# Attention, two expert layers: the query tiles of the second batch loaded as 32 by 32 squares and transposed on VectorE

## The chip, the core and the metric

The kernel runs on one core of a Trainium2 chip. The metric is the device time of one execution in microseconds (us). Below, PE is TensorE (matmuls and transposes through the identity matrix), PEld its weight loads, DVE is VectorE, ACT is ScalarE, POOL is GpSimd, and SP is SyncE, the engine from whose queue all loads and stores are issued.

## What is computed

A block-sparse attention over q, k, v of shape (2, 8, 768, 64) is followed by a mixture of eight experts with Sinkhorn-normalised gates and by a second layer with a rational activation. The change lies in the attention alone:

```python
k_sum = k.reshape(B, H, nb, block, D).max(axis=3)          # block = 32
v_sum = v.reshape(B, H, nb, block, D).mean(axis=3)
scores_l = scale * np.matmul(q, k.transpose(0, 1, 3, 2))   # kept where |i - j| < 16
scores_s = scale * np.einsum('bhsd,bhnd->bhsn', q, k_sum) + np.log(block)
a = softmax(np.concatenate([scores_l_masked, scores_s], axis=-1))
attn = np.matmul(a, np.concatenate([v, v_sum], axis=2))
x = attn.transpose(0, 2, 1, 3).reshape(B * S, H * D)
x = _moe_ref(x, w_gate, w1, w2)
return _moe2_ref(x, w_in, w_out, a, b)
```

All is float32, and `scale` is 1/8.

## The kernel before

**Steps.** The attention goes through 24 steps `t` (`NQ`), each 64 queries of all 8 heads; steps 0 to 11 are the first batch, 12 to 23 the second. A step has five pieces, issued at different times: `scores(t)` (q times k on PE, lines 626 and 637), `exps(t)` (ACT), `norm(t)` (DVE), `trans(t)` (PE transposes the weights, line 668; ACT copies them, line 670) and `values(t)` (weights times v, line 687). Up to step 11 the loop takes one step at a time and ends it with `values(t - 3)`; from step 12 on `pair(s)` takes two, with `values(s - 4)` and `values(s - 3)` directly behind the scores of `s` and `s + 1`. So `values(14)` and `values(15)` stand in pair 18.

**Between the pieces** stand pieces of the first expert unit's matmuls (`main`, lines 184 to 186) and whatever the table `todo` lists for the step: `at(s, f, ...)` puts `f` into step `s`. Every engine, SP too, takes its instructions in the order in which this code issues them; nothing is reordered.

**The v rows of a step** come through `load_vx(t)` into one of three buffers `vx[t % 3]`. It is issued when `values(t - 3)` has read that buffer. In pair 16, after `values(12)` and `values(13)`, this loads the rows of steps 15 and 16.

**A query tile** is 256 tokens of one batch, four steps' worth: (b, i) with i from 0 to 2. PE wants it with the 64 head dimensions on the partitions, two heads to a 128-row slab, four slabs: `qs`, 128 by 4 by 256. Before, a tile of the second batch is loaded by `load_tok` in two DMAs (even and odd tokens, rows of 64 floats), and `prep_q` makes eight PE transposes into two PSUM buffers of tag "tr" (`transpose8`, line 427) and copies both out with the scale 1/8 (`place`, lines 438 and 440: one on ACT, one on DVE). Tile (1, 0) is loaded with step 7 into `accs` and prepared with step 10, (1, 1) with steps 11 and 14, (1, 2) with steps 15 and 18:

```python
at(11, load_tok, q, "q", 1, 1)
at(15, load_tok, q, "q", 1, 2)
at(7, load_tok, q, "q", 1, 0, 0)
order += [(j * TPL - 2, "q", j // NL, j % NL) for j in range(2, NQ // TPL)]
```

The keys are prepared in the same way by `prep_k`, from tiles that POOL has first rewritten by token (`by_token`, line 388).

Of the kernel before, what the change touches and what calls it, by code (L numbers as in the profile page):

```python
# [10 lines left out]
F32 = mybir.dt.float32  # L11
# [11 lines left out]
def kernel(  # L23
# [14 lines left out]
    nc = tc.nc  # L38
    B, H, S, D = q.shape
    NT, DM = out.shape  # L40
    NE, _, FE = w1.shape
    F2 = w_out.shape[0]
    P = 128
# [18 lines left out]
    NP = H // 2  # L62
    LT = 2 * P
    NL = S // LT
# [30 lines left out]
    accs = xpool.tile([P, NTT, DM], F32, name="accs")  # L95
# [270 lines left out]
    with ExitStack() as actx:  # L366
        apool = actx.enter_context(tc.tile_pool(name="att", bufs=2, side="right"))
# [11 lines left out]
        nat = {}  # L379
        kT = {}  # L380
        ks = {}
        vs = {}
        qT = {}
# [34 lines left out]
        def transpose8(nm, b, i, par, early=False):  # L418

            t = nat[nm, b, i]  # L420
            name = f"{nm}ps_{b}_{i}_{par}"
            if early or par:
                ps = psm.tile([P, NP * P], F32, tag="mm", name=name).rearrange("p (c n) -> p c n", c=NP)
            else:
                ps = psa.tile([P, NP, P], F32, tag="tr", name=name, bufs=2)
            for p in range(NP):
                nc.tensor.transpose(ps[:, p, :], t[par][:, p * P:(p + 1) * P], ident)
            return ps

        def place(dst, par, ps, mul, early=False):  # L430

            if len(dst.shape) == 4:
                o = dst.rearrange("p s c (n t) -> p s c n t", t=2)[:, :, :, :, par]
                ps = ps.rearrange("p c (s n) -> p s c n", s=TPL)
            else:
                o = dst.rearrange("p c (n t) -> p c n t", t=2)[:, :, :, par]
            if par and not early:
                nc.vector.tensor_scalar_mul(o, ps, mul)
            else:
                nc.scalar.mul(o, ps, mul)  # L440
# [28 lines left out]
        def new_k(b, i):  # L469
            a = slot(b * QB + i * TPL)  # L470
            kT[b, i] = kw[:, a:a + TPL, :, WIN:WIN + QT]
            if i == 0:
                ks[b] = apool.tile([P, NP, NB], F32, tag="ks", name=f"ks_{b}")

        def new_q(b, i):
            qT[b, i] = qs[(b * NL + i) % 2]
# [19 lines left out]
            nc.vector.tensor_max(o, o, m)  # L496

        qscale = 1.0 / math.sqrt(D)

        ordered = []  # L500

# [23 lines left out]
        def prep_k(b, i):  # L525
            new_k(b, i)
            for par in range(2):
                place(kT[b, i], par, transpose8("k", b, i, par), 1.0, i == 0)

        def prep_q(b, i):  # L530
            new_q(b, i)
            for par in range(2):
                place(qT[b, i], par, transpose8("q", b, i, par), qscale, (b, i) == (0, 2))

# [264 lines left out]
        def at(s, f, *args):  # L799
            todo.setdefault(s, []).append(lambda: f(*args))  # L800
# [19 lines left out]
        at(5, by_token, "q", 0, 2)  # L820
        for i in range(NL):
            at(6 + i, by_token, "k", 1, i)
        at(11, load_tok, q, "q", 1, 1)
        at(15, load_tok, q, "q", 1, 2)
        at(7, load_nat, v, "v", 1, 0)
        at(8, load_nat, v, "v", 1, 1)
        at(9, load_nat, v, "v", 1, 2, 8)
        at(5, dma_w, 0, 2, 0, 6)
        at(7, dma_w, 0, 2, 1)
        at(7, load_tok, q, "q", 1, 0, 0)  # L830
        for t in range(1, 3):
            at(3, block_values, t)
        order = [(7 + i, "k", 1, i) for i in range(NL)]
# [2 lines left out]
        for t, nm, b_, i_ in order:  # L836
            at(t, prep_q if nm == "q" else prep_k, b_, i_)
# [72 lines left out]
        for s in range(PAIR):  # L910
# [11 lines left out]
            if s == AV:  # L922
                trans(1)
                exps(3)
                norm(2)
                prep_v(0, 2)
                prep_q(0, 1)
# [111 lines left out]
    for src, dst in ((w_in, f_in), (w_out, f_out)):  # L1039
        rows, cols = dst[0].shape[0] // P, dst[0].shape[1]  # L1040
        flat, o = rows * cols, 0
        while o < flat:
            e = min(o + CW, flat)
            parts = []
            while o < e:
                r, c = divmod(o, cols)
# [458 lines left out]
```

## Time and profile before

| what | before |
|---|---|
| median of 3 runs (lowest to highest) | 1350.45 us (1350.25 to 1350.63) |
| the profiled execution, its time | 1350.37 us |
| its span, first to last instruction | 1348.7 us |
| PE busy | 1340.8 us, 99% of the span |
| DVE, ACT, POOL busy | 1050.1, 510.6, 803.1 us |
| granted TensorE clock | 1.00 |
| chain that ended last | PE 97%, DVE 1%, ACT 1%, DMA 1% |

Busy time is the time in which an engine had an instruction under way, from first to last of them merged. The chain is followed back from the last instruction, at each step to what released it. The profiled execution lasted 1.67 us longer than its span (what lies before the first and behind the last instruction), and its time is 0.08 us under the median.

### The profile page before, as it was taken

The numbers are of one execution on the slowest core, as the hardware profiler recorded it, in microseconds if no ns is written. First come the engines' busy times: TensorE is split into PE (matmuls) and PEld (weight loads), VectorE is DVE, ScalarE is ACT, GpSimd is POOL, SyncE is SP. The second block draws the span as 40 slices with busy tenths as digits, with TensorE's granted clock in tenths as the row PEclk, the third lists the DMA queues.
The fourth block names the chain that finished last, engine by engine and source line by source line (L and its number), as shares of the span: only waits on it lengthen the run. The fifth ranks groups of instructions, "written<-read, shape, count | busy, mean of one in ns | idle before, by whom it ended". The sixth has DMA issues, their size and how long they took to land.

```text
span 1348.7 us, 20280 instructions
## 1 busy us (share of the span) xinstructions
PE 1340.8 (99%) x7343; PEld 1186.2 (88%) x7343; DVE 1050.1 (78%) x1956; ACT 510.6 (38%) x1136; POOL 803.1 (60%) x983
## 2 busy tenths in 40 slices
PE   8999999999999999999999999999999999999999
PEld 6888898999899999899999999999999888888887
DVE  7766588777777777777787777777777689988885
ACT  7875213222222222222222222222222379866662
POOL 7625747777767777777777767777777012222221
PEclk9999999999999999999999999999999999999999
DMA  9730112222222222222222222222221411312102
GB/s 263 169 85 1 63 35 73 78 77 73 68 73 68 69 76 69 83 70 85 69 81 67 71 70 68 77 68 83 68 86 56 146 60 45 94 33 94 32 16 78
DMA packets 122004, 102.40 MB, mean 76 GB/s; under 512 B 36272, under 2 KB 102960, under 8 KB 121904
## 3 DMA queue, kind: packets, MB, share of 16 engines
q1 hardware_dynamic: 121904, 101.10, 25.4%
q8 instruction: 58, 0.95, 0.3%
q14 instruction: 42, 0.34, 0.1%
HBM read 81.15 MB, written 19.92 MB: 75 GB/s over the span
## 4 chain that ended last, share of the span: by engine, by line
PE 97%; DVE 1%; ACT 1%; DMA 1%; SPq 0%; issue 0%; POOL 0%; DVEq 0%
PE p_v L185 12%; PE p_v L184 12%; PE p_v L186 12%; PE p L184 8%; PE p L186 8%; PE p L185 8%; PE X L1280 6%; PE X L1278 6%; PE X L1279 6%; PE Z L1280 3%; PE Z L1279 3%; PE Z L1278 3%; PE Y L1280 2%; PE Y L1279 2%; PE Y L1278 2%; PE xo L687 1%
## 5 line engine op out<-in xcount | busy, mean ns | idle before, releaser
L1393 DVE SCALAR_TENSOR_TENSOR accs<-p_v,Pt,accs 128x512 f32<-128x512 f32 x336 | 244.2, 745 | 86.8 <-PE p_v L186 86.0
L184 PE MATMUL p_v<-w2h_v,hh_v 128*128 128x512 f32 x720 | 282.0, 392 | 0.1
L186 PE MATMUL p_v<-w2h_v,hl_v 128*128 128x512 f32 x720 | 281.7, 391 | 0.0
L185 PE MATMUL p_v<-w2l_v,hh_v 128*128 128x512 f32 x720 | 281.6, 391 | 0.0
L1287 DVE SCALAR_TENSOR_TENSOR hl_v<-s,hh_v 128x384 fp32r<-128x384 f32 x180 | 135.9, 755 | 76.1 <-ACT hh_v L1286 74.6
L234 POOL TENSOR_TENSOR hl<-ta,hh 128x512 fp32r<-128x512 f32 x48 | 62.4, 1300 | 204.5 <-ACT hh L233 153.1
L1298 ACT COPY s<-X 128x384 f32<-128x384 f32 x56 | 27.0, 483 | 407.5 <-PE X L1280 407.5
L1087 POOL TENSOR_SCALAR ce<-ce 128x296 uint32<-128x296 uint32 (+1 forms) x56 | 67.1, 1199 | 177.5 <-DVE ce L1078 177.5
L186 PEld LDWEIGHTS p_v<-w2h_v,hl_v 128*128 128x128 f32 x720 | 135.1, 188 | 28.4
L184 PEld LDWEIGHTS p_v<-w2h_v,hh_v 128*128 128x128 f32 x720 | 135.4, 188 | 26.4 <-DVE accs L1388 0.5
L185 PEld LDWEIGHTS p_v<-w2l_v,hh_v 128*128 128x128 f32 x720 | 135.2, 188 | 26.1
L1286 ACT ACTIVATE hh_v<-s 128x384 fp32r<-128x384 f32 x180 | 94.9, 527 | 125.9 <-DVE s L1321 67.8
L110 POOL TENSOR_TENSOR wS<-S,wS 128x256 fp32r<-128x256 f32 x120 | 100.2, 835 | 14.4 <-ACT wS L107 4.7
L184 PE MATMUL p<-xh,w1h 128*128 128x512 f32 (+2 forms) x272 | 101.2, 372 | 0.0
L186 PE MATMUL p<-xh,w1l 128*128 128x512 f32 (+2 forms) x272 | 99.1, 364 | 0.0
L185 PE MATMUL p<-xl,w1h 128*128 128x512 f32 (+2 forms) x272 | 99.0, 364 | 0.0
L184 PE MATMUL p<-w2h,hh 128*128 128x512 f32 (+1 forms) x240 | 94.2, 393 | 0.0
L186 PE MATMUL p<-w2h,hl 128*128 128x512 f32 (+1 forms) x240 | 93.3, 389 | 0.0
L185 PE MATMUL p<-w2l,hh 128*128 128x512 f32 (+1 forms) x240 | 93.1, 388 | 0.0
L110 POOL TENSOR_TENSOR w2l_v<-sb,w2h_v 128x512 fp32r<-128x512 f32 x60 | 82.8, 1380 | 5.0
L1280 PE MATMUL X<-th,wS 128*128 128x384 f32 x240 | 80.3, 334 | 0.0
L1279 PE MATMUL X<-tl,wS 128*128 128x384 f32 x240 | 80.3, 334 | 0.0
(252 smaller groups left out, 3302.5 us busy)
## 6 DMA issues: line engine op xcount, KB each, us to landing
sa<-in_moe_w_dram SPq DMA_DIRECT2D x30, 512.0 KB, 3.4
sb<-in_moe_w_dram SPq DMA_DIRECT2D x30, 512.0 KB, 4.3
cv<-in_moe_w_in_dram SPq DMA_DIRECT2D x24, 296.0 KB, 2.9
w1h<-f_in SPq DMA_DIRECT2D x16, 256.0 KB, 2.8
w1l<-f_in SPq DMA_DIRECT2D x16, 256.0 KB, 3.2
w2h<-f_out SPq DMA_DIRECT2D x16, 256.0 KB, 4.4
w2l<-f_out SPq DMA_DIRECT2D x16, 256.0 KB, 4.9
vx<-in_v_dram SPq DMA_DIRECT2D x20, 192.0 KB, 4.4
```

Of the source, the lines that this page charges most:

```text
L110: nc.gpsimd.tensor_sub(lo, src, hi.bitcast(F32))
L184: nc.tensor.matmul(ps, lhsT=sh, rhs=mh, start=(i == 0), stop=False)
L185: nc.tensor.matmul(ps, lhsT=sh, rhs=ml, start=False, stop=False)
L186: nc.tensor.matmul(ps, lhsT=sl, rhs=mh, start=False, stop=(i == n_k - 1))
L234: nc.gpsimd.tensor_sub(hl[:, :n], ta, hh[:, :n].bitcast(F32))
L1087: nc.gpsimd.tensor_scalar(out=e, in0=e, scalar1=896, scalar2=0, op0=ALU.subtract, op1=ALU.max)
L1278: nc.tensor.matmul(ps, lhsT=w[:, 0, t], rhs=mh, start=start and t == 0, stop=False, **go)
L1279: nc.tensor.matmul(ps, lhsT=w[:, 0, t], rhs=ml, start=False, stop=False, **go)
L1280: nc.tensor.matmul(ps, lhsT=w[:, 1, t], rhs=mh, start=False, stop=t == 1, **go)
L1286: nc.scalar.activation(hh, src, AF.Relu)
L1287: nc.vector.scalar_tensor_tensor(out=hl, in0=src, scalar=0.0, in1=hh.bitcast(F32), op0=ALU.max, op1=ALU.subtract)
L1393: nc.vector.scalar_tensor_tensor(out=a, in0=ps, scalar=Pt[:, g, e:e + 1], in1=a, op0=ALU.mult, op1=ALU.add)
```

## The change

The query tiles (1, 0), (1, 1) and (1, 2) are now loaded by `load_squares`, in 16 DMAs each. One DMA takes 32 head dimensions of one head and 256 tokens and puts token r of every group of 32 on partition r: the tile in SBUF consists of squares of 32 tokens by 32 dimensions, each already standing at the place where its transpose belongs. `prep_q` turns them all with one `nc.vector.transpose` of 128 by 1024 into `qs`; the eight PE transposes, the two PSUM buffers and the two copies go. That instruction has no scale, so the 1/8 moves to the keys of the second batch, whose copies have a factor already. Tiles (1, 1) and (1, 2) are loaded with steps 11 and 15 as before; the four quarters of (1, 0), four DMAs each, with steps 5, 6, 7 and 8, into the same part of `accs`.

```diff
+        squares = tuple((1, i) for i in range(NL))
@@ prep_k
-                place(kT[b, i], par, transpose8("k", b, i, par), 1.0, i == 0)
+                place(kT[b, i], par, transpose8("k", b, i, par), qscale, i == 0)
+        def load_squares(src, nm, b, i, place=None, parts=range(4)):
+            if place is None:
+                t = apool.tile([P, NP, LT // SQ, SQ], F32, tag="nat", name=f"{nm}_{b}_{i}", bufs=3)
+            else:
+                t = accs[:, place:place + 2, :].rearrange("p a f -> p (a f)")
+                t = t.rearrange("p (c n r) -> p c n r", c=NP, r=SQ)
+            s = src[b, :, i * LT:(i + 1) * LT, :]
+            for y in parts:
+                h, c = divmod(y * SQ, D)
+                for p in range(NP):
+                    nc.sync.dma_start(
+                        t[y * SQ:(y + 1) * SQ, p],
+                        s[2 * p + h, :, c:c + SQ].rearrange("(n r) c -> r n c", r=SQ),
+                    )
+            nat[nm, b, i] = t.rearrange("p c n r -> p c (n r)")
@@ prep_q
+            if (b, i) in squares:
+                nc.vector.transpose(qT[b, i], nat.pop(("q", b, i)))
+                return
@@ the table
-        at(11, load_tok, q, "q", 1, 1)
-        at(15, load_tok, q, "q", 1, 2)
+        at(11, load_squares, q, "q", 1, 1)
+        at(15, load_squares, q, "q", 1, 2)
-        at(7, load_tok, q, "q", 1, 0, 0)
+        for y in range(P // SQ):
+            at(5 + y, load_squares, q, "q", 1, 0, 0, (y,))
```

**SP's queue around tile (1, 2).** `vx_104`, `vx_105` and `vx_103` are the three v buffers; the first two rows here are steps 13 and 14, and the `vx_103` behind `sb` is step 15. `sa` and `sb` are weights of the experts. Before:

```order
L600 DMA vx_104<-in_v_dram 96x8x64
L600 DMA vx_105<-in_v_dram 96x8x64
L339 DMA sa_1208<-in_moe_w_dram 128x4x256
L397 DMA q_2_1230<-in_q_dram 128x8x64 x2
L342 DMA sb_1238<-in_moe_w_dram 128x2x512
L600 DMA vx_103<-in_v_dram 96x8x64
```

And now:

```order
L621 DMA vx_104<-in_v_dram 96x8x64
L621 DMA vx_105<-in_v_dram 96x8x64
L339 DMA sa_1214<-in_moe_w_dram 128x4x256
L542 DMA q_2_1236<-in_q_dram 32x8x32 x16
L342 DMA sb_1258<-in_moe_w_dram 128x2x512
L621 DMA vx_103<-in_v_dram 96x8x64
```

The order is the same; between `sa` and `sb` stand sixteen issues in place of two.

**SP's queue around tile (1, 0)**, steps 5 to 8 of the changed kernel (`k_2` is the key tile (1, 2), `v_0` and `v_1` are value tiles, `s_0_1` weights):

```order
L542 DMA accs<-in_q_dram 32x8x32 x4
L621 DMA vx_103<-in_v_dram 96x8x64
L415 DMA k_2_583<-in_k_dram 128x8x128
L542 DMA accs<-in_q_dram 32x8x32 x4
L621 DMA vx_104<-in_v_dram 96x8x64
L415 DMA v_0_657<-in_v_dram 128x8x128
L132 DMA s_0_1_659<-in_moe_w_dram 128x2x512
L542 DMA accs<-in_q_dram 32x8x32 x4
L621 DMA vx_105<-in_v_dram 96x8x64
L415 DMA v_1_742<-in_v_dram 128x8x128
L542 DMA accs<-in_q_dram 32x8x32 x4
```

Before, two DMAs of 128x8x64 stood behind `s_0_1`, and the four groups of squares were not there.

**DVE in pair 18**, one piece of the difference (the `xo` and `a` rows are `norm`, the `ISA` row is the first of the next scores):

```order
-L662 TENSOR_TENSOR a_1368<-a_1368,xo_1403 128x480
-L438 TENSOR_SCALAR qs_107<-qps_2_1_1450 128x512
-L637 ISA a_1486,sm_1487<-sc_1477,mask_111 128x120
+L683 TENSOR_TENSOR a_1388<-a_1388,xo_1423 128x480
+L551 STREAM_TRANSPOSE qs_107<-q_2_1236 128x1024
+L658 ISA a_1495,sm_1496<-sc_1486,mask_111 128x120
```

The transpose of a whole tile stands where DVE's half of the copy stood; ACT's half is gone without a successor. Tiles (1, 0) and (1, 1) look alike.

## Rows read from the trace of the kernel before

**Rows 1.** Busy time of each engine by stretches; columns are named in the first line.
```profile
core 0: us, PE busy (x) PEld busy (x) DVE busy (x) ACT busy (x) POOL busy (x), PEclk, DMA share, GB/s
32.00:48.00 16.00, 16.00 (x216) 14.57 (x212) 13.73 (x57) 15.51 (x55) 11.61 (x18) 1.00 1.08 262
48.00:100.00 52.00, 51.94 (x674) 44.55 (x670) 36.34 (x174) 40.74 (x158) 20.14 (x25) 1.00 0.40 93
140.00:1040.00 900.00, 899.89 (x4530) 815.38 (x4529) 699.60 (x1204) 217.86 (x475) 659.87 (x805) 1.00 0.23 71
```

**Rows 2.** The longest wait of PE: who, for whom, us, times, longest.
```profile
PE spin L540 <- POOL ident masks.py:199: 1.4, 1, 1.4
```

**Rows 3.** The chain that ended last, at the tiles' transposes: start, us, piece.
```profile
45.92 0.87 PE qps L427 x8
...
64.53 0.87 PE qps L427 x8
...
79.26 0.87 PE qps L427 x8
```

**Rows 4.** The same chain in pair 18: scores, then values 14 and 15.
```profile
73.46 1.30 PE sc L626 x32
74.77 1.08 PE xo L687 x32
```

**Rows 5.** SP's issues in time, 49 to 75 us: start, us, line, what, count.
```profile
49.16 1.09 SPq L397 DMA_DIRECT2D q<-in_q_dram  x2
...
53.76 0.33 SPq L600 DMA_DIRECT2D vx<-in_v_dram  x1
54.14 0.55 SPq L346 DMA_DIRECT2D wgr<-in_moe_w_gate_dram  x1
54.74 0.53 SPq L347 DMA_DIRECT2D coef<-in_moe_a_dram  x1
55.31 0.43 SPq L348 DMA_DIRECT2D coef<-in_moe_b_dram  x1
...
64.96 1.08 SPq L397 DMA_DIRECT2D q<-in_q_dram  x2
66.15 2.07 SPq L342 DMA_DIRECT2D sb<-in_moe_w_dram  x1
68.90 6.84 SPq L600 DMA_DIRECT2D vx<-in_v_dram  x3
```

**Rows 6.** v rows of steps 15 and 16: issue, and time to landing.
```profile
L600 SPq DMA_DIRECT2D vx<-in_v_dram x1: 330/330/330, 68.9 to 68.9; - x1
...
DMA to landing us min/median/max: 3.9/3.9/3.9
...
L600 SPq DMA_DIRECT2D vx<-in_v_dram x1: 442/442/442, 69.4 to 69.4; - x1
...
DMA to landing us min/median/max: 5.0/5.0/5.0
```

**Rows 7.** Issues from 54.1 to 56 us: KB each, median us to landing.
```profile
wgr<-in_moe_w_gate_dram SPq DMA_DIRECT2D x1, 16.0 KB, 2.5
coef<-in_moe_a_dram SPq DMA_DIRECT2D x1, 2.0 KB, 2.7
coef<-in_moe_b_dram SPq DMA_DIRECT2D x1, 1.0 KB, 3.3
```

**Rows 8.** Key tile (1, 2): landing of the DMA issued at 30.0, POOL, the chain.
```profile
DMA to landing us min/median/max: 7.2/7.2/7.2
...
37.53 1.20 POOL L388 TENSOR_SCALAR accs<-k 128x512 f32<-128x512 f32 x2
...
41.81 0.87 PE kps L427 x8
```

**Rows 9.** DVE in time at the copy of tile (1, 0); idle before in brackets.
```profile
47.59 1.21 DVE L480 TENSOR_REDUCE ks<-kw 128x32 f32<-128x1024 f32 x1
48.72 0.68 DVE L438 TENSOR_SCALAR qs<-qps 128x512 f32<-128x512 f32 x1
...
52.76 0.28 DVE L637 CUSTOM_DVE_ANT_0 a<-sc,mask 128x120 f32<-128x120 f32 x1 [0.91 <-PE sc L626]
```

More of the change, by code (lines that the diff above doesn't have):

```diff
@@ L498 @@
         qscale = 1.0 / math.sqrt(D)
+        SQ = 32
+        squares = tuple((1, i) for i in range(NL))
         ordered = []
```

## The prediction

> **What bounds the kernel now.** I read the busy times by stretch first. PE is busy in all of 16.00, 51.94 of 52 and 899.89 of 900 us of three stretches, at a granted clock of 1.00, so from 32 us on the time is the sum of what PE executes, and work taken from PE or a wait given to it moves the end one for one [rows 1]. Then the chain that ended last: it goes through the transposes of the three tiles, with nothing between them and their neighbours [rows 3]. Then SP's queue in time, because the change turns 6 issues into 48 on it, and in it stand the v rows which PE reads [rows 5, 6]. The same view by stretch says where DMA has room: share 1.08 from 32 to 48 us, that is, full; 0.40 on average from 48 to 100 [rows 1].
>
> **What goes.** 24 PE transposes, eight for each of three tiles. Each group holds the chain for 0.87 us [rows 3]: 3 x 0.87 = 2.61 us, all on the path. 2.61 us is 0.19% of the time; a measurement of this kernel can tell about 0.2%, or 2.7 us, from no change. So even the whole gain would lie at the edge of what can be told.
>
> ACT loses three copies and DVE three of 0.68 us [rows 9]; neither engine holds the chain there, so this is counted at nothing. The factor 1/8 on the keys rides on copies that exist.
>
> **What comes on DVE.** Three transposes of 128 by 1024. The trace has none. From below they can't cost less than nothing beside the 0.68 us that goes; the nearest row is the reduction that also streams 128 by 1024, 1.21 us [rows 9]; from above I take twice that, 2.4 us. I use 1.21: DVE works 0.53 us longer at each tile. At tile (1, 0), where DVE is fullest, it idles 0.91 us before the next scores reach it [rows 9], so 0.53 is covered; at 2.4 us some 0.8 us would run over into the next step, whose weights PE wants only two steps later. Cost on the path 0.
>
> **What comes on SP, tile (1, 0).** Four groups of four squares stand between the loads of steps 5 to 8, where the DMA engines are full. An issue there costs at least what it costs in the idle stretch: `wgr` and both `coef` loads, 16, 2 and 1 KB, run back to back from 54.14 to 55.74, 1.60 us for three, or 0.53 each, whatever their size; the pair of large query loads takes 1.08, or 0.54 each [rows 5]. Key tile (1, 2) is now behind four squares, 4 x 0.53 = 2.1 us later: it was issued at 30.0 and landed after 7.2, so 39.3 instead of 37.2; POOL needs 1.20 to rewrite it, and PE takes it at 41.81 [rows 8]. That leaves 1.3 us. The bytes are the same, in twice as many pieces; the v rows of these steps are used three steps after their issue. I take 0 on the path. For the upper end: four groups less the pair that goes are 8.5 - 1.1 = 7.4 us more of SP over four steps, 1.9 a step, 0.6 more than the key tile's 1.3 us of room; I call it 1 us.
>
> **What comes on SP, tile (1, 1).** SP came to its loads at 49.16 [rows 5]; sixteen issues take 16 x 0.53 = 8.5 us, to 57.7. Behind them stand the v rows of step 12, which PE wants in pair 16, after 67 us. Cost 0.
>
> **What comes on SP, tile (1, 2).** Here I see the price. Before, its two loads start at 64.96 and `sb` follows at 66.15; the v rows of step 15 go out at 68.90, released by `values(12)`, and land 3.9 us later, at 72.8 [rows 5, 6]. PE begins values 14 and 15 at 74.77, 1.08 us for both, so `values(15)` at 74.77 + 0.54 = 75.31 [rows 4]. That is 2.5 us to spare. Now:
> - the loads start one removed group earlier: 64.96 - 0.87 = 64.09;
> - sixteen issues at 0.53 end at 64.09 + 8.5 = 72.6;
> - `sb` takes one more, to 73.1 (the 2.07 us of before I read as a wait for full DMA engines; squares issued one in 0.53 us don't fill them);
> - the v rows of step 15 go out at 73.1 and land 3.9 us later, again behind `sb`: 77.0;
> - PE is there 2 x 0.87 us earlier than before, at 75.31 - 1.74 = 73.6.
>
> PE waits 77.0 - 73.6 = 3.4 us. The tile itself lands about 75.5, before DVE's turn near 80. The v rows of steps 16 to 18 come right behind and are wanted a pair later: no further wait.
>
> Bounds. Shortest issue: a lone one lasts 0.33 us, and `wgr` starts 0.38 after the issue before it [rows 5]. With 0.38 the sixteen end at 70.2, `sb` at 70.6, the rows land at 74.5, and PE waits 0.9. If the landing were only the 2.7 of a small load [rows 7], 73.3, there is no wait at all. Longest: `coef` starts 0.60 after `wgr` [rows 5]; the sixteen end at 73.7, `sb` at 74.3, and with the 5.0 us of the next v load [rows 6] the rows land at 79.3: PE waits 5.7. I take 0.53, as the mean of the only three small loads in a row.
>
> **Sum.** -2.61 + 0 + 0 + 3.4 = +0.8 on the profiled execution's 1350.37, so 1351.2 us; the median of the runs is 0.08 higher, which I leave aside.
>
> **A rule against the change.** The landings show that small loads overlap: three issued 0.6 us apart land 2.5 to 3.3 us after their own issue, not one after the other [rows 7]. The Trainium skill, page "DMA: Bandwidth & Descriptors", section "Rules for kernel authors", wants many small transfers coalesced and says that under 64 KB one pays mostly overhead; a square DMA is 32 KB, and the same page gives some 2 us as each transfer's fixed cost. If that cost were paid in turn, sixteen would take 32 us instead of 8.5, an estimate from that page, and the time would be near 1375; by the landings only the issue is paid in turn. I give that case one in a hundred, inside the slower rival.
>
> **Rivals.**
> 1. *No wait for the v rows.* The issues are as short as the shortest, or a square, with fewer pieces than any load around it, is issued faster than I think; the rows land before 73.6. For: single issues of 0.33 us. Against: three small loads in a row, one of 1 KB among them, still cost 0.53 each. Time: 1350.37 - 2.61 = 1347.8; with the 0.9 us wait of the short bound 1348.7. Chance 0.18, half of it faster by over 0.2%.
> 2. *Slower: the wait is long.* One mechanism, SP's queue before the v rows of step 15. It decides once they land after 78.9, for then the wait exceeds 2.61 + 2.7 = 5.3 us. That needs 0.60 an issue and a landing near 5.0: 5.7 - 2.6 = +3.1, 1353.5; with 1 us from tile (1, 0), 1354.5. What may add to it: PE's longest wait so far is 1.4 us, and the granted clock is 1.00 in every stretch [rows 1, 2], so the trace doesn't say what an idle time of 3 to 6 us does to the clock. If it fell to 1.2 GHz for 4 us afterwards, PE would lose 2 us more, and the forecast's wait would be enough: 1353.2. The Trainium skill, page "TensorE: Matmul & The Clock Gate", Part 1, says that an idle TensorE is put back to 1.2 GHz; no row here shows it. Chance 0.18.
> 3. *The change doesn't do what it says*: squares that spread over few DMA engines would land late, and DVE would wait instead of PE. Each transpose waits for all its sixteen loads, and DVE turns to tile (1, 0) near 48.7 us [rows 9]. If it landed a few us after that, DVE's 0.91 us of idle time would be gone and PE would get its weights late, by what is beyond: to come out slower it would have to land after 54. I count this within rival 2's chance.
>
> **How the numbers follow.** Forecast, a wait of 1 to 5.3 us and a change between -1.6 and +2.7: 0.64, all within 0.2%. Rival 1: 0.18, of which 0.09 faster and 0.09 the same. Rivals 2 and 3: 0.18, slower. So faster 0.09, same 0.73, slower 0.18. The range reaches from the full gain, 1347.8, to between rival 2's two ends, 1354.0.
>
> **What would show it.** On PE, in the chain and the waits: three groups of eight transposes gone; a wait of 2 to 5 us inside the values of pair 18 (line 687, line 708 of the changed file), ended by a DMA, near 73.6 us. On SP: sixteen issues of about 0.53 us from 64 to 72.6, and the v load at 73. On DVE: transposes near 1.2 us that wait for nothing. Wrong would be: issues under 0.4 us, a v load landed before 73.6, PE waiting at another place in steps 8 to 12, or a granted clock under 1.00 after the wait.

## The result, and the profile after

| what | before | changed |
|---|---|---|
| median of 6 runs each (lowest to highest) | 1350.53 us (1350.25 to 1350.67) | 1357.11 us (1356.10 to 1359.76) |
| ratio of the times | | 1.0051, 95% interval 1.0039 to 1.0064 |
| the profiled execution, its time | 1350.37 us | 1356.17 us |
| its span | 1348.7 us | 1354.5 us |
| mean granted clock of the span | 1.00 | 0.998 |

The changed kernel is slower by 0.51%, 6.6 us in the medians and 5.8 us in the two profiled executions. The forecast of 1351.2 us and its range, up to 1354.0, are missed. The loss is looked for with the same views as before.

The stretches first, with the columns of [rows 1]; the last of them ends at 1046 us, where 1040 stood before.

```profile
32.00:48.00 16.00, 15.19 (x208) 13.68 (x203) 13.42 (x57) 15.16 (x53) 11.15 (x17) 1.00 1.00 221
48.00:100.00 52.00, 46.06 (x596) 39.26 (x596) 36.06 (x169) 36.04 (x144) 20.49 (x26) 0.97 0.49 104
100.00:140.00 40.00, 39.83 (x244) 34.74 (x245) 22.74 (x44) 21.06 (x54) 17.57 (x19) 1.00 0.02 5
140.00:1046.00 906.00, 905.89 (x4561) 820.77 (x4560) 700.62 (x1210) 220.17 (x482) 666.27 (x811) 1.00 0.24 71
```

PE, which idled 0.06 us from 48 to 100 us, now idles 5.94 us there and 0.81 us from 32 to 48, where it idled 0.00; from 100 to 1046 it idles 0.28 us, 0.23 before. Between 48 and 100 us the clock's mean is 0.97, not 1.00. So whatever happened lies in the attention, and in two kinds: idle time, and a slower clock.

The waits of PE (who, for whom, us in total, times, longest) name the idle time. Waits that the kernel before has too are left out, but for the longest of them [rows 2], and so are two of 0.4 and 0.2 us in the first 8 us: PE's next wait there ends at 9.34 us, where it ended at 9.39 before, so they delay nothing.

```profile
PE xo L708 <- DMA vx<-in_v_dram: 4.8, 1, 4.8
PE spin L561 <- POOL ident masks.py:199: 1.4, 1, 1.4
PE xo L708 <- ACT a L668: 1.0, 1, 1.0
...
PE sc L647 <- DVE qs L551: 0.7, 1, 0.7
...
PE p L186 <- DVE hl L263: 0.3, 1, 0.3
```

In time, on PE (start, us, line, what; in brackets the idle time before it and who ended it):

```profile
48.15 0.69 PE L708 MATMUL xo<-aT,vx 120*64 120x64 f32 x16 [0.96 <-ACT a L668]
...
52.33 0.50 PE L186 MATMUL p<-w2h,hl 128*128 128x512 f32 x1 [0.32 <-DVE hl L263]
...
67.78 1.05 PE L647 MATMUL sc<-kw,qs 64*64 64x120 f32 x32 [0.68 <-DVE qs L551]
...
73.70 1.37 PE L647 MATMUL sc<-kw,qs 64*64 64x120 f32 x32
75.00 0.69 PE L708 MATMUL xo<-aT,vx 120*64 120x64 f32 x16
80.48 1.12 PE L708 MATMUL xo<-aT,vx 120*64 120x64 f32 x16 [4.79 <-DMA vx<-in_v_dram]
81.53 0.80 PE L184 MATMUL p<-w2h,hh 128*128 128x512 f32 x1
```

The last four rows are pair 18: `values(14)` runs to 75.69, then PE stands for 4.79 us in front of `values(15)`, for the v rows of step 15. The same sixteen matmuls as at 75.00 then take 1.12 us in place of 0.69. The other three waits, 0.96 + 0.32 + 0.68 = 1.96 us, lie around the tiles (1, 0) and (1, 1).

What those v rows waited for stands on SP's queue in time, from tile (1, 1) on, and in the chain that ended last:

```profile
49.35 10.75 SPq L542 DMA_DIRECT2D q<-in_q_dram  x16
...
62.75 0.91 SPq L621 DMA_DIRECT2D vx<-in_v_dram  x2
63.75 0.49 SPq L339 DMA_DIRECT2D sa<-in_moe_w_dram  x1
64.33 10.89 SPq L542 DMA_DIRECT2D q<-in_q_dram  x16
75.33 0.39 SPq L342 DMA_DIRECT2D sb<-in_moe_w_dram  x1
75.82 1.87 SPq L621 DMA_DIRECT2D vx<-in_v_dram  x3
```

```profile
75.33 0.39 SPq L342
...
75.82 4.52 DMA vx<-in_v_dram
...
80.48 1.12 PE xo L708 x16
```

In the place of [rows 5] the sixteen issues last 10.89 us, the v rows go out at 75.82 and land at 80.35. The chain, which went through PE alone in pair 18 [rows 4], now passes through SP's queue and this DMA.

The clock behind the wait, by stretches of the changed kernel (columns as in rows 1):

```profile
80.48:83.50 3.02, 3.02 (x21) 2.52 (x22) 1.58 (x5) 0.37 (x1) 0.00 (x0) 0.50 0.39 88
83.60:87.00 3.40, 3.40 (x19) 2.79 (x18) 2.26 (x5) 1.07 (x2) 0.00 (x0) 1.00 0.00 1
```

From 80.48 to 83.50 the granted clock is 0.50, that is 1.2 GHz, directly after the one long idle time of the kernel; then it is 2.4 GHz again. Everywhere else in the kernel, waits of 1.4 us and less left it at 1.00. The profiled execution is one of the two shortest. The other five show a mean clock of 0.997 or 0.996, and the two with 0.996 are the longest, 1358.47 and 1359.76 us; so the clock probably cost more there than in the trace, which may be why the medians differ by 6.6 us and the profiled executions by 5.8. It was not traced.

DVE's transposes themselves came as taken (all of line 551: ns least/median/most, first and last start):

```profile
L551 DVE STREAM_TRANSPOSE qs<-q x2: 1236/1236/1237, 66.5 to 84.7; 128x1024 f32<-128x1024 f32 x2
...
L551 DVE STREAM_TRANSPOSE qs<-accs x1: 1245/1245/1245, 49.6 to 49.6; 128x1024 f32<-128x1024 f32 x1
```

1.24 us each, where 1.21 was used from the reduction of the same shape [rows 9].

### The profile page after: what moved, and what is told of

The parts are those of the page before. It is cut to its first block, busy times and chain, and to the rows that moved or that the text cites. A ratio compares the mean times of both kernels' runs of the same rounds, so it can differ in the third digit from the quotient of the medians.

```text
span 1354.5 us, 20277 instructions
## 1 busy us (share of the span) xinstructions
PE 1339.3 (99%) x7319; PEld 1183.8 (87%) x7319; DVE 1050.3 (78%) x1956; ACT 509.6 (38%) x1133; POOL 803.8 (59%) x983
## 4 chain that ended last, share of the span: by engine, by line
PE 92%; DVE 1%; DMA 0%; ACT 0%; issue 0%; SPq 0%
PE p_v L185 12%; PE p_v L186 12%; PE p_v L184 12%; PE p L184 8%; PE p L186 8%; PE p L185 8%; PE X L1302 6%; PE X L1300 6%; PE X L1301 6%; PE Z L1302 3%; PE Z L1301 3%; PE Z L1300 3%; PE Y L1302 2%; PE Y L1301 2%; PE Y L1300 2%; PE x L1052 0%
```

## Experiments

The theory after the first look: of the 5.8 us, the wait for the v rows is 4.8, the clock's fall 1.3 to 1.5, the small waits at tiles (1, 0) and (1, 1) 1.96, less the 2.61 that went. Its rivals: each tile's share is about the same, as it would be if DVE or the many DMAs as such cost the time; and, for the slow matmuls behind the wait, a cause other than the clock.

**One tile at a time: (1, 2).** The other two tiles are loaded and transposed as before. (Not shown: the copies of these two tiles have the factor 1, since the 1/8 stays with the keys.)

```diff
-        squares = tuple((1, i) for i in range(NL))
+        squares = ((1, 2),)
-        at(11, load_squares, q, "q", 1, 1)
+        at(11, load_tok, q, "q", 1, 1)
-        for y in range(P // SQ):
-            at(5 + y, load_squares, q, "q", 1, 0, 0, (y,))
+        at(7, load_tok, q, "q", 1, 0, 0)
```

> Only tile (1, 2) is in squares; tiles (1, 0) and (1, 1) are loaded and transposed as before. Theory (SP's queue: the sixteen issues hold back the v rows of step 15, PE idles for them, and its clock falls): nearly the whole loss is here, a wait of 4.5 to 6 us inside the values of pair 18, a granted clock of 0.5 for some 3 us after it, 1.5 us more, less 0.87 us of transposes: 1355 to 1357 us. Rival (each tile's 4,096 pieces of 128 B, or its transpose on DVE, cost by themselves, in equal parts): a third of the loss of 6.6 us, about 1352.7 us.

Measured: 1355.49 us against 1350.44, ratio 1.0036 (1.0025 to 1.0048). PE in pair 18:

```profile
74.76 0.69 PE L708 MATMUL xo<-aT,vx 120*64 120x64 f32 x16
79.64 0.69 PE L708 MATMUL xo<-aT,vx 120*64 120x64 f32 x16 [4.19 <-DMA vx<-in_v_dram]
```

One tile of the three brings 5.05 of the 6.6 us: the equal shares are out. The clock fell here too, a little after the wait (0.66 on average from 79.6 to 82.5 us, 0.79 from there to 86).

**Tile (1, 0) alone, and tile (1, 1) alone**, by the same edit with `squares = ((1, 0),)` and `((1, 1),)`.

> Only tile (1, 0) is in squares, in four parts with steps 5 to 8. Theory (SP's queue before the v rows of step 15): these issues come long before; PE gains 0.87 us and gives 0.9 to 1.3 back in steps 10 to 12, because weights and v rows land up to 3.5 us later: 1350.3 to 1351.2 us. Rival (equal parts): about 1352.7 us.

> Only tile (1, 1) is in squares. Theory: PE gains 0.87 us and may wait up to 0.7 us for the transpose on DVE before the scores of pair 16: 1349.7 to 1350.5 us. Rival (equal parts): about 1352.7 us.

Measured: (1, 0) 1351.09 us, ratio 1.0005 (0.9996 to 1.0014); (1, 1) 1349.99 us, ratio 0.9997 (0.9988 to 1.0006). The waits of PE at their places, of the first and of the second kernel:

```profile
PE xo L708 <- ACT a L668: 0.7, 1, 0.7
...
PE p L186 <- DVE hl L263: 0.4, 1, 0.4
```

```profile
PE sc L647 <- DVE qs L551: 0.7, 1, 0.7
```

So tile (1, 0) waits a little longer than it saves, 0.74 + 0.41 against 0.87 us, and tile (1, 1) a little less, 0.68 against 0.87. The three tiles alone add up to 0.65 - 0.45 + 5.05 = 5.25 us of the 6.6 for all; the rest, 1.3 us, lies within the spread of the changed kernel's executions, 1356.10 to 1359.76.

**The weights out of the way.** `sa` and `sb`, 512 KB each, are issued with step 17 instead of 14 and 15; the sixteen squares stay before the v rows.

```diff
-        at(14, dma_sub, 0, 1)
-        at(15, dma_sub, 0, 2)
+        at(17, dma_sub, 0, 1)
+        at(17, dma_sub, 0, 2)
```

> The change, with the two loads of expert weights, one just ahead of the squares of tile (1, 2) and one just behind, put two or three steps later; the sixteen issues stay where they are. Theory: the v rows of step 15 go out 1 to 2 us earlier and land after 2.7 us instead of 4.5, since nothing large is in front of them; the wait shrinks from 4.8 to 1 or 2 us and the clock holds: 1351 to 1353 us. Rival (the sixteen issues alone make the whole wait): 1355 us or more.

Measured: 1351.05 us, ratio 1.0006 (0.9997 to 1.0015). SP's queue in time:

```profile
63.65 8.47 SPq L542 DMA_DIRECT2D q<-in_q_dram  x16
72.22 2.30 SPq L621 DMA_DIRECT2D vx<-in_v_dram  x2
```

The v rows of step 15 go out at 72.22 and land at 75.62, 3.4 us later; PE waits 0.15 us and the clock stays at 1.00. Two issues taken out ahead of the v rows, with 1 MB of traffic, bring them 4.7 us sooner: 3.6 in the queue, 1.1 in the landing. Of the 3.6 the two issues themselves are 1.2; the other 2.4 is that the sixteen now last 8.47 us in place of 10.89. So the loss is not in the squares as such. It is in the queue ahead of this one load, and the weights beside the squares are part of it. They were moved together: what each of them did is not shown.

**The squares behind the v rows.** Tile (1, 2) is loaded with step 16 instead of 15, and nothing else is changed.

```diff
-        at(15, load_squares, q, "q", 1, 2)
+        at(16, load_squares, q, "q", 1, 2)
```

> The change with one number altered: the squares of tile (1, 2) are loaded with step 16, so behind the v rows of steps 15 and 16 in SP's queue, not before them. Theory: the wait of 4.8 us in pair 18 and the fall of the clock go, 6.3 us; the tile itself lands near 79 us, and up to 2 us of that may come back as a wait for it before the scores of pair 20: 1350.5 to 1353 us. Rival (equal parts, wherever the loads stand): 1357 us as before.

Measured: 1352.55 us, ratio 1.0012 (1.0003 to 1.0022). The wait for the v rows is gone; instead the tile itself is late:

```profile
74.79 1.15 PE L708 MATMUL xo<-aT,vx 120*64 120x64 f32 x32
82.56 1.05 PE L647 MATMUL sc<-kw,qs 64*64 64x120 f32 x32 [1.41 <-DVE qs L551]
```

The time is moved from one wait to another, 1.41 us long, and most of the loss is gone. Of ten executions four took 1350.3 to 1350.7 and six 1352.4 to 1353.7; the profiled one, 1350.66, is of the four. All four show a mean clock of 1.00, five of the six 0.998 or 0.999, so a fall of the clock seems to be part of the difference; none of the six was traced.

**Is the clock a cause of its own?** Matmuls without use between `values(14)` and `values(15)`, into the PSUM tile that `values(15)` then overwrites, so that PE does not idle there. First forty:

```diff
+            if t == 15:
+                for _ in range(40):
+                    nc.tensor.matmul(ps[:, 0, 0:QT], lhsT=ident, rhs=ident[:, 0:QT], start=True, stop=True)
```

> The change, with 40 small matmuls of the identity matrix put on PE between the values of step 14 and of step 15, into the PSUM tile that those of step 15 overwrite (nothing of the result changes). By the rows of the kernel before (three of the 128-column ones hold the chain for 0.67 us) they keep PE at work for some 4.5 us, about the length of its wait. Theory (the idle PE loses its clock, and that costs 1.5 us behind the wait): the clock stays at 1.00 and the time comes to 1355 to 1356.3 us. Rival (the fall of the clock costs nothing that counts, or has another cause): 1357 us as before, or more.

Measured: 1358.71 us against 1350.39. The expectation missed: the forty took 9.03 us, 0.23 each, twice what I had worked out, and PE ran 4 us past the landing of the rows. The clock did stay at 1.00, but the time says little. So again, with twenty (`range(20)`):

> The changed kernel with twenty added matmuls of the identity (64 columns, into the PSUM tile that values 15 then overwrites) between values 14 and values 15 of pair 18. In the run with forty, 40 took 9.03 us, 0.226 us each; so twenty take 4.5 us and end at 75.7 + 4.5 = 80.2 us, as the v rows of step 15 land (80.1 to 80.4). Theory (part of the loss is the clock, which fell to 0.5 after the idle 4.8 us): PE idles under 1 us there, the granted clock stays 1.00, and from the start of values 15 to the end the program is 1.3 to 1.5 us shorter than in the changed kernel: 1357.1 - 1.4 = 1355.7 us. Rival (the slower rows behind the wait have another cause, such as the late loads or the values themselves, and the clock figure only goes along with it): the slow stretch behind 80 us stays, 1357.1 us or more.

Measured: 1355.55 us (1354.28 to 1358.67), ratio 1.0045 (1.0031 to 1.0059). PE waits 0.2 us in place of 4.8. The stretch from the start of `values(15)` over the same 21 matmuls, first with the twenty, then in the changed kernel:

```profile
79.91:81.73 1.82, 1.82 (x21) 1.57 (x22) 0.96 (x4) 0.00 (x0) 0.00 (x0) 1.00 0.35 79
```

```profile
80.48:83.60 3.12, 3.12 (x21) 2.62 (x22) 1.68 (x5) 0.37 (x1) 0.00 (x0) 0.51 0.39 89
```

Both kernels read the same v rows out of the same loads. At 1.00 the stretch takes 1.82 us, at 0.51 it takes 3.12: 1.30 us. From the start of `values(15)` to the end of the span it is 1352.6 - 79.91 = 1272.7 us with the twenty, 1354.5 - 80.48 = 1274.0 without: 1.3 us again. The kernel with forty, in which `values(15)` starts at 84.29, says the same: 1356.9 - 84.29 = 1272.6. The medians go the same way, 1.6 us less for a kernel that executes twenty matmuls more, though the intervals of the two ratios overlap. Three of its five executions kept a mean clock of 1.00 and took 1354.3 to 1355.6 us; the two with 0.998 and 0.997 took 1357.8 and 1358.7. So the rival falls: the slow stretch is the clock's, and its price in the traced executions is 1.3 us.

**Three tiles, with the queue arranged.** `sa` and `sb` with step 17, and of tile (1, 2) three quarters with step 14 and the last with step 16. (Not shown: the lines for `sa` and `sb`, as above, and those that put both pieces into one tile.)

```diff
-        at(15, load_squares, q, "q", 1, 2)
+        at(14, load_squares, q, "q", 1, 2, None, range(3))
+        at(16, load_squares, q, "q", 1, 2, None, (3,))
```

> All three tiles in squares, the two weight loads later as in the run before, and tile (1, 2) in two pieces: three quarters with step 14, before the v rows of step 15 are free to be loaded, the last quarter with step 16, behind them. Theory: no wait for v rows; the 2.61 us of transposes less 0.96 + 0.32 us of waits that tile (1, 0) brought in steps 11 and 12 and 0.68 us for the transpose of tile (1, 1): 1349.4 to 1350.4 us. Rival (squares cost by themselves): above 1352 us.

Measured: 1350.26 us, ratio 0.9999 (0.9989 to 1.0008). Three waits remain, 1.11 + 0.67 + 0.56 = 2.3 us, against the 2.61 that went:

```profile
PE p L186 <- DVE hl L263: 1.1, 1, 1.1
...
PE sc L650 <- DVE qs L554: 0.7, 1, 0.7
...
PE xo L711 <- ACT a L671: 0.6, 1, 0.6
```

All three are at tiles (1, 0) and (1, 1), and two of them come from DVE.

**Two tiles.** Tile (1, 0) as before the change; the queue as in the last kernel; and each transpose in two halves of 128 tokens, the second one step later, since the first scores want only the first half. (Not shown: the lines for the queue and for tile (1, 0), as in the kernels above.)

```diff
-        squares = tuple((1, i) for i in range(NL))
+        squares = ((1, 1), (1, 2))
-                nc.vector.transpose(qT[b, i], nat.pop(("q", b, i)))
+                x = nat[("q", b, i)]
+                half = lambda z: nc.vector.transpose(qT[b, i][:, :, z * P:(z + 1) * P], x[:, :, z * P:(z + 1) * P])
+                half(0)
+                at((b * NL + i) * TPL - 1, half, 1)
```

> As the run before, but tile (1, 0) is loaded and transposed on PE as before the change, and the transposes of the other two tiles on DVE are cut into halves of 128 tokens, so that the scores of pair 16 wait for half of one. Theory: 2 x 0.87 us of transposes go and at most 0.3 us comes back: 1348.7 to 1349.4 us, the fastest version. Rival: 1350 us or more, if the wait behind tile (1, 1) isn't the length of its transpose.

Measured: 1348.66 us (1348.45 to 1349.93), ratio 0.9988 (0.9978 to 0.9997). The halves on DVE, and two stretches:

```profile
L555 DVE STREAM_TRANSPOSE qs<-q x4: 668/696/703, 66.0 to 79.2; 128x512 f32<-128x512 f32 x4
```

```profile
32.00:48.00 16.00, 16.00 (x220) 14.71 (x220) 13.73 (x57) 15.35 (x55) 11.60 (x18) 1.00 1.06 256
48.00:100.00 52.00, 51.69 (x688) 44.05 (x677) 37.99 (x177) 40.80 (x159) 20.74 (x26) 1.00 0.44 94
```

A half takes 0.70 us, about what DVE's half of the copy took before [rows 9]. PE is busy in 16.00 and 51.69 us of these stretches, 16.00 and 51.94 before the change, and the two groups of transposes that went, 2 x 0.87 = 1.74 us, appear nearly whole: 1.7 us less in the medians, 1.6 in the spans of the profiled executions (1347.1 against 1348.7). This version beats both kernels, the one before by 0.12%. So the squares do pay, for the tiles whose loads and whose DVE work find room. The kernel before with nothing but `sa` and `sb` moved was not run; PE had no wait there that this could have removed.

## Why the prediction was wrong

The prediction's own sum and what the profiled executions show (the clock by the experiment with twenty matmuls):

| term | predicted, us | measured, us |
|---|---|---|
| 24 transposes on PE gone | -2.61 | -2.61 |
| DVE's transposes (tiles (1, 1), (1, 2)) | 0 | 0.68 |
| SP and DVE at tile (1, 0) | 0, at most 1 | 0.96 + 0.32 |
| SP at tile (1, 1) | 0 | 0 |
| wait for the v rows of step 15 | 3.4 | 4.79 |
| clock | 0 (in a rival: 2) | 1.3 |
| sum | +0.8 | +5.4, of 5.8 in the span |

The measured column says where PE stood idle or slow, not what each cause would cost by itself: what PE lost ahead of `values(15)` it would otherwise have spent there, in front of the v rows. Along the path, `values(15)` starts at 80.48 us and not at 75.31 (74.77 + 0.54, [rows 4]), 5.17 later; the third group of transposes, behind it, gives 0.87 back, and the clock takes 1.3: 5.6 of the 5.8 us. So two things make the miss: the v rows landed at 80.35 and not at 77.0, 3.35 us late, and the clock's 1.3. Together they are 4.65 of the 5.0 us between the forecast's +0.8 and the measured +5.8.

Two of the signs that the prediction named for being wrong are there: PE waiting at other places in steps 8 to 12, and a granted clock under 1.00 after the wait. The other two are not: one issue of the sixteen is under 0.4 us, and the v rows did not land before 73.6.

**What was right.** Where the time would be lost, and through what: SP's queue, `sb`, then the v rows in pair 18. The DVE transposes, 1.24 us for 1.21. SP came to the tile at 64.33 where 64.09 was forecast, but this was luck, two errors that cancel: SP reached the v loads ahead of `sa` at 62.75, 1.6 us later than 62.04 - 0.87, and these two then took 0.91 us in place of 2.25. Squares overlap in flight: they land a median of 3.1 us after their issue, and sixteen issues take 10.9 us. By the estimate made from the Trainium skill, page "DMA: Bandwidth & Descriptors" (section "Rules for kernel authors", and the page's some 2 us for each transfer, which it fits to DMAs issued from POOL), they would have taken 32 with that cost paid in turn; this trace does not show it paid in turn, though small transfers did turn out dear here, by their issues. And as rival 2 had it, the clock fell after an idle time of 3 to 6 us, and added to the loss.

**The step that failed first is the size of one term: "sixteen issues at 0.53 end at 64.09 + 8.5 = 72.6".** They lasted 10.89 us and ended at 75.22. This is 2.4 of the 3.35 us; the landing behind them is 0.6, SP's start 0.24. The steady issue is shorter than taken, not longer: 0.45 us and 0.04 to the next. But three of the sixteen last 1.2 to 1.3 us, and one is held until an earlier load has landed. The squares' issues in three stretches of SP's queue, 65.6 to 67.2, 71.2 to 73.0 and 73.0 to 75.3 us (ns least/median/most, first and last start):

```profile
L542 SPq DMA_DIRECT2D q<-in_q_dram x3: 442/1222/1342, 64.3 to 66.2; - x3
...
L542 SPq DMA_DIRECT2D q<-in_q_dram x5: 448/449/450, 71.0 to 73.0; - x5
...
L542 SPq DMA_DIRECT2D q<-in_q_dram x3: 449/451/1258, 73.0 to 74.8; - x3
```

The hold is plainest in the chain of the kernel with twenty added matmuls (start, us, what), where the load issued at 64.04 has to land first:

```profile
64.04 6.09 DMA q<-in_q_dram
...
70.14 0.31 SPq L542
...
70.50 0.45 SPq L542
```

In the changed kernel the hold is for `sa`, issued at 63.75 and landed at 70.14; the issue behind it starts at 70.16. Among the waits of SP's queue (us, times, longest):

```profile
SPq L542 <- DMA sa<-in_moe_w_dram: 0.7, 1, 0.7
```

In both kernels the load that has to land stands eight issues ahead of the one that is held. So 16 x 0.49 + 3 x 0.8 + 0.7 = 10.9 us. With `sa` and `sb` out of the way the sixteen lasted 8.47 us, one of them long and none held, which is the forecast's 8.5: it fits squares with no large load close ahead of them, as the rows that it was taken from had none. The forecast took a mean of three quiet issues and even its upper bound, 0.60, allowed for no long one, though the trace of before has them: two v loads there take 2.25 us together, just ahead of the tile.

```profile
62.04 2.25 SPq L600 DMA_DIRECT2D vx<-in_v_dram  x2
```

The landing, 3.9 us by [rows 6], was 4.5. Together the rows came at 80.35, not 77.0, past the 78.9 that rival 2 gave as its point of decision.

**The second failure is two costs put at nothing.** For tile (1, 1) the step reads "At tile (1, 0), where DVE is fullest": only that tile was looked at. At (1, 1) the scores of step 16 stand right behind the tile's last instruction. Before, ACT and DVE made half of the copy each; now DVE makes the whole alone, from 66.48 to 67.72, and PE's scores begin at 67.78 after 0.68 us of waiting. For tile (1, 0) the step named key tile (1, 2) as the one that could be late. It was, by 3.0 us (landed at 40.14), and PE took it without a new wait. What cost time was a later load of the same queue, the weights `s_0_1`, landed at 44.85 and not at 41.39. ACT waits for them:

```profile
44.87 1.15 ACT L107 CAST w2h<-s 128x512 fp32r<-128x512 f32 x2 [0.35 <-DMA s<-in_moe_w_dram]
```

Then ACT comes to `xh` at 45.92, DVE's `xl` waits for that, `norm(9)` behind it ends at 48.05, and PE's values start at 48.15. Before, `norm(9)` ended at 47.67 and PE came at 48.01, with 0.3 us to spare. The profile names ACT's line 668 for this wait; the row through `norm` is read from the times, and only that it belongs to tile (1, 0) is shown, by the kernel with that tile alone. And DVE's turn to the tile itself waits for its loads, 0.40 us, after which `hl` comes 0.32 late to PE:

```profile
49.58 1.25 DVE L551 STREAM_TRANSPOSE qs<-accs 128x1024 f32<-128x1024 f32 x1 [0.40 <-DMA accs<-in_q_dram]
```

These waits also made PE reach `values(15)` at 75.69 instead of 73.6, and so hid part of the first error: had PE been there on time, and the rows no earlier, it would have waited 80.35 - 73.6 = 6.7 us. So in the changed kernel itself this failure cost little; with the other two mended it decides, as in the three-tile kernel with the queue arranged, whose 2.3 us of waits eat the gain.

**The third failure is the clock,** which stood in a rival, at 2 us and 0.18 together with the long wait. The forecast's own wait of 3.4 us lay inside the 3 to 6 us for which it said that the trace shows nothing; a term for it belonged in the sum's upper end for the forecast too. The 2 us of that rival supposed a low clock for 4 us; the price here was 1.3. On the rule cited there, the Trainium skill, page "TensorE: Matmul & The Clock Gate", Part 1, that an idle TensorE is put back to 1.2 GHz, this trace agrees: 0.50 from 80.48 to 83.50 us after 4.79 us of idling.

The first failure, with the fall of the clock that follows from its wait, makes the loss by itself: tile (1, 2) alone brought 5.05 us. By the table 0.4 of the 5.8 us stay unassigned, along the path 0.2.

## What to carry to other kernels

Price a group of DMAs by what stands behind it on its in-order queue: issues times their time, long ones and holds included, against the slack of the next load that the bounding engine reads. When work moves from a bounding engine to another, look at the slack at every place where it lands, not only at the one that seems fullest. Waits on one path do not simply add up: one in front of a longer wait may cost nothing until the longer one is gone. A wait of 4 to 5 us on TensorE cost its length and 1.3 us more here.

## What the runs showed of the hardware

- Back to back, an issue on SP lasts here about the same whatever it moves: 0.45 us for a square of 32 KB in 128-byte pieces, 0.49 for `sa` and 0.39 for `sb`, 512 KB each, and 0.04 us from one square to the next. It can be longer: before the change `sb` took 2.07 us [rows 5], at a DMA share of 1.07 over that issue.
- Of the long issues of squares some begin as a 16-KB instruction load runs. From 73.35 to 74.75 us in the changed kernel, with the DMA engines a third busy, the one long issue (1.26 us, at 73.47) and one such load stand side by side (the queue's row: packets, MB, share of 16 engines):

```profile
q8 instruction: 1, 0.02, 4.1%
```

  Whether the load lengthens the issue was not tried; the first square of each group, at 49.35 and 64.33, is long without one.
- A useless matmul of 64 columns against the 128 by 128 identity takes 0.23 us and shows as two records: the twenty stand there as 40, with 4.7 us in all. I had expected 0.11, half of what the expectation above takes for one of 128 columns (three of them in 0.67 us).
